# Attention followed by a mixture of experts: earlier row reads, weights in smaller pieces, and a sort that is cut differently

## The chip, the cores and the metric

One core of a Trainium2 chip. The metric is the device time of one execution in microseconds, lower is better. Times of a kernel are the median of several executions; the profile is one more execution with the hardware profiler on.

## What is computed

Two blocks after each other, all in float32: attention over 8 batches, 8 heads, 576 positions and 64 dimensions, with a causal mask and a bias from the running sum of `s`; then a mixture of 8 experts over the 4608 tokens of 512 elements that this gives. A token takes the expert of its own highest logit, or, where its local gate is at least 0.5, that of the token before.

```python
scores = scale * np.matmul(q, k.transpose(0, 1, 3, 2))
cum = np.cumsum(np.maximum(s, 0.0), axis=-1)
bias = -(cum[:, :, :, None] - cum[:, :, None, :])
scores = np.where(causal, -1e9, scores + np.minimum(bias, 0.0))
attn = softmax(scores)                       # exp, over its sum + 1e-9
x = matmul(attn, v)                          # to (B, S, 512)
logits = x @ w_gate                          # 8 experts
gate = sigmoid(x @ w_local)
for b, s:                                    # in order along s
    e = argmax(logits[b, s]) if s == 0 or gate[b, s] < 0.5 else prev_e
    prev_e = e
    p = softmax(logits[b, s])
    out[b, s] = p[e] * (np.maximum(x[b, s] @ w1[e], 0.0) @ w2[e])
```

## The kernel before

**Attention.** 32 steps, one for each pair of heads (n = 0 to 31, four for each batch), and a 33rd that ends the last. In step n TensorE computes the scores of pair n (L307, L313), ScalarE their exponentials (L318, L329), GpSimd the causal mask in place (L324, L331), and TensorE the values of pair n-1 (L359, L371, L375). The values carry nine more columns, so that logits and local gate come out of the same matmuls. VectorE divides by the sums and writes the token rows of the batch to the tiles `xb` and `xt` in SBUF (L365, L378). Loads of the batches are issued on SyncE's queue; `store` (L381) moves the rows of the last 64 positions of a batch into place, on the same queue.

**The sort.** The tokens have to be brought together by expert. `Group` does this for several batches at once, in five stages (choose, rows, hold, rank, gates), which give each token a row number in the DRAM tensor `x_rows`; then one indirect DMA from GpSimd for each 128 tokens (five a batch, the last with 64) scatters the rows there (L937). `plan` says after which half step of the attention each stage and scatter is issued: batches 0 to 2 from step 13, 3 to 5 from step 25, three scatters a half step. `Sort.early` (step 27) then fills the gap behind the rows so far of experts 0 to 3 with empty rows: their first 128 rows each can be worked on before the sort is finished. The last two batches are sorted after the attention, while the first blocks of the experts run: their stages and scatters are `hooks` (L112), which `experts` calls after so many groups of matmuls. `fill` (L767) writes 128 empty rows behind each expert's rows, eight DMAs on SyncE's queue, and `tables` computes which expert and which first row each further block has.

**The experts.** 41 blocks of up to 128 rows: 4 early ones and 37 further ones. Block i needs its rows (`xg`, 257 KB, read by GpSimd's queue, L999 for the early ones, L1003 else), which TensorE transposes (L1010, `turn_x`) and VectorE copies (L1012), and the two weight matrices of its expert (`w`, two loads of 2 MB on SyncE's queue, L947, 16 KB a partition each). Layer 1 is 32 matmuls of 128x128 (L1027; each matmul shows as two records), layer 2 is 8 of 128x512 (L1039). ScalarE and VectorE apply the relu, VectorE multiplies by the gate (`y`, L1044), and GpSimd scatters y to the output (L1045). There are three weight buffers: the first is allocated ahead of the attention, so that the first block's weights are loaded during it (step 20); the other two lie where the attention's tiles were. `xg` has four buffers.

Each engine works through its instructions in program order. The loop of the blocks sets that order:

```python
for i in range(NBL):
    load(i + 2)              # SyncE: weights
    layer1(i + 1, 0)
    fetch(i + 2)             # GpSimd: rows
    layer1(i + 1, 1)
    layer2(i)                # turn_x(i + 2) in its middle, the store of y at its end
```

So GpSimd's queue holds: store of block i-1, read of rows i+2, store of block i, read of rows i+3. A load of weights waits on SyncE's queue until TensorE has read the buffer for the last time. All stores go to one tensor, so each waits for the one before it to land.

Of the kernel before, what the change touches and what calls it, by code (L numbers as in the profile page):

```python
# [10 lines left out]
F32 = mybir.dt.float32  # L11
# [7 lines left out]
P = 128  # L19
# [32 lines left out]
@with_exitstack  # L52
def kernel(
    ctx: ExitStack,
    tc: tile.TileContext,
    q: bass.AP,
    k: bass.AP,
    vm: bass.AP,
    vt: bass.AP,
    vT: bass.AP,  # L60
    s: bass.AP,
    w_gate: bass.AP,
    w_local: bass.AP,
    w1: bass.AP,
    w2: bass.AP,
    out: bass.AP,
):
# [12 lines left out]
    recs = const.tile([P, NPAIR, 2 * NF + 1], F32, name="recs")  # L80
    out_of = const.tile([P, 1], I32, name="out_of")
    sort = Sort(tc, const, lg, rows_d, ident)

    with ExitStack() as main:
        keep = main.enter_context(tc.tile_pool(name="keep", bufs=4))
        wf = main.enter_context(tc.tile_pool(name="wf", bufs=1))
        xs = {}

        def new_x(b):
            xs[b] = keep.tile([P, NF, XW], F32, name="xb"), keep.tile([TL, XW], F32, name="xt")  # L90
            return xs[b]


        plan = {}

        def at(n, half, *what):
            plan.setdefault((n, half), []).extend(what)

        for bs, n0, each in (((0, 1, 2), 13, 3), ((3, 4, 5), 25, 3)):
            g = sort.group(bs, xs)  # L100
            for i, (n, half) in enumerate(((n0, 1), (n0 + 1, 0), (n0 + 1, 1), (n0 + 2, 0), (n0 + 2, 1))):
                at(n, half, g.stages[i])
            for i, f in enumerate(g.scatters):
# [12 lines left out]
        experts(tc, w1, w2, out, rows_d, ident, sort,  # L116
                [("early", e) for e in range(EARLY)] + [("further", i) for i in range(SURE)], hooks, wf, first)
    total = nc.values_load(sort.total[0:1, 0:1], min_val=0, max_val=NBLK,  # L118
                           skip_runtime_bounds_check_because="a count of blocks")
    with tc.If(total > SURE):  # L120
        experts(tc, w1, w2, out, rows_d, ident, sort, [("further", i) for i in range(SURE, SURE + 2)])
        with tc.If(total > SURE + 2):
            experts(tc, w1, w2, out, rows_d, ident, sort, [("further", i) for i in range(SURE + 2, NBLK)])
    wrong = nc.values_load(out_of[0:1, 0:1], min_val=0, max_val=P * NPAIR * (2 * NF + 1),
                           skip_runtime_bounds_check_because="a count of elements")
    with tc.If(wrong > 0):
        attention_general(tc, q, k, vm, vt, s, w_gate, w_local, cum_d, x_d, ident, lg)
        with ExitStack() as again:
            pool = again.enter_context(tc.tile_pool(name="again", bufs=1))
            ps = again.enter_context(tc.tile_pool(name="again_ps", bufs=3, space=PSUM))  # L130

            def bank(n):
                return [ps.tile([P, 512], F32, name="bank") for _ in range(n)]

            sort = Sort(tc, pool, lg, rows_d, ident)
            sort.constants(bank)
            for bs in (range(0, 4), range(4, 8)):
                xs = {b: (pool.tile([P, NF, XW], F32, name=f"xb{b % 4}"), pool.tile([TL, XW], F32, name=f"xt{b % 4}"))
                      for b in bs}
                for b in bs:  # L140
                    r0 = b * S
# [11 lines left out]
def attention(ctx, tc, q, k, vm, vt, vT, s, w_gate, w_local, ident, lg, recs, keep, new_x, plan):  # L153
# [787 lines left out]


def load_weights(nc, w, w1, w2, e):
    for a, src in ((0, w1), (DK * F, w2)):
        n = DK * F if src is w1 else FK * D
        s = src[e : e + 1] if isinstance(e, int) else src[bass.ds(e, 1)]
        nc.sync.dma_start(w[:, a : a + n], s.rearrange("o p c f -> (o p) (c f)"))  # L947


@with_exitstack  # L950
def experts(ctx, tc, w1, w2, out, rows_d, ident, sort, blocks, hooks=(), wf=None, first=None):

# [19 lines left out]
    ws, xg, at, xT, hT = {0: first} if wf else {}, {}, {}, {}, {}  # L972

    def bank(n):
        return [ps_r.tile([P, 512], F32, name="bank") for _ in range(n)]
# [17 lines left out]
    def fetch(i):  # L993
        if i >= NBL or i in xg:
            return
        kind, j = blocks[i]
        xg[i] = gp.tile([P, XW], F32, name="xg")
        if kind == "early":
            nc.gpsimd.dma_start(xg[i], rows_d[j * R : j * R + P, :])  # L999
        else:  # L1000
            row = nc.values_load(sort.rowi[0:1, j : j + 1], engines=[ET.Pool], min_val=0, max_val=E * R,  # L1001
                                 skip_runtime_bounds_check_because="a block's first row")
            nc.gpsimd.dma_start(xg[i], rows_d[bass.ds(row, P), :])  # L1003

    def turn_x(i):
        if i >= NBL:
# [27 lines left out]
    def layer2(i):  # L1034
        ps = ps_y.tile([P, D], F32, name="yp")
        h = hT.pop(i)
        w = ws[i][:, DK * F :].rearrange("p (c d) -> p c d", c=FK)
        for c in range(FK):
            mm(ps, lhsT=h[:, c, :], rhs=w[:, c, :], start=(c == 0), stop=(c == FK - 1))  # L1039
# [4 lines left out]
        nc.vector.tensor_scalar_mul(y, ps, xg[i][:, D + 1 : D + 2])  # L1044
        nc.gpsimd.indirect_dma_start(  # L1045
            out=out[:, :], out_offset=bass.IndirectOffsetOnAxis(ap=at[i][:, 0:1], axis=0),
            in_=y[:, :], element_offset=0, bounds_check=N - 1, oob_is_err=False, in_offset=None)

    for i, (kind, _) in enumerate(blocks):
        if kind == "early" or i < 2:  # L1050
            fetch(i)
    load(0)
    load(1)
    turn_x(0)
# [47 lines left out]
```

## Time and profile before

Median of three runs 1109.63 us (1104.3 to 1112.8). The profiled execution spans 1120.1 us, with a mean granted TensorE clock of 0.951.

| engine | busy, us | share of the span |
|---|---|---|
| TensorE matmuls | 968.3 | 86% |
| TensorE weight loads (beside the matmuls) | 710.3 | 63% |
| VectorE | 210.6 | 19% |
| ScalarE | 181.8 | 16% |
| GpSimd | 173.9 | 16% |

| DMA issue | count | KB each | median us to landing |
|---|---|---|---|
| expert weights | 82 | 2048 | 13.5 |
| row reads | 41 | 257 | 11.4 |
| stores of y (indirect) | 41 | | 8.7 |
| scatters of full tiles (indirect) | 32 | | 3.7 |

A row of the busy view by stretches gives for each engine the time in which it had an instruction running; the rest of the stretch is idle. The granted clock is the share of full speed that TensorE was given. In the view of waits, a line names the engine and line that stood still, what ended the wait, and the total, the number of times and the longest. In the timeline, the brackets hold the idle time of the engine just before the row and what ended it.

### The profile page before, as it was taken

How to read it: one execution, taken by the hardware profiler on the slowest of the kernel's cores; microseconds unless marked ns; L12 is line 12 of the kernel's file. 1: busy time of each engine (PE TensorE's matmuls, PEld its weight loads, DVE VectorE, ACT ScalarE, POOL GpSimd, SP SyncE). 2: the span in 40 equal slices, each digit the busy share in tenths (PEclk: the TensorE clock that was granted, in tenths of full speed). 3: DMA queues.
4: the chain of work that ended last, by engine and by line, in shares of the span. 5: the costliest groups of instructions: out<-in, count | busy, mean ns of one | idle time of the engine just before them, and what ended most of it. 6: DMA issues, size and time to landing. Idle time of an engine off the chain costs nothing.

```text
span 1120.1 us, 16042 instructions
## 1 busy us (share of the span) xinstructions
PE 968.3 (86%) x6538; PEld 710.3 (63%) x6538; DVE 210.6 (19%) x649; ACT 181.8 (16%) x465; POOL 173.9 (16%) x333
## 2 busy tenths in 40 slices
PE   8999998999989978888888787878888897879785
PEld 6778877777877645565556565656555564646462
DVE  3222352223424211111111111111111111111110
ACT  4444444445530000000000000000000000000000
POOL 2212215312451211010001010101000010101000
PEclk9999999999998989999999999899999888999898
DMA  9435436653229965857575757575757475766640
GB/s 281 134 115 175 148 89 208 261 159 114 95 87 362 349 268 192 322 202 285 199 318 198 308 203 298 194 308 197 295 195 310 183 267 235 264 243 246 252 180 18
DMA packets 42646, 245.24 MB, mean 219 GB/s; under 512 B 17309, under 2 KB 17341, under 8 KB 29376
## 3 DMA queue, kind: packets, MB, share of 16 engines
q1 hardware_dynamic: 31024, 213.36, 51.2%
q0 software_dynamic: 9632, 29.73, 7.1%
q10 hardware_dynamic: 1904, 0.98, 0.3%
q8 instruction: 56, 0.92, 0.3%
q14 instruction: 30, 0.25, 0.1%
HBM read 220.67 MB, written 23.64 MB: 218 GB/s over the span
## 4 chain that ended last, share of the span: by engine, by line
issue 33%; DMA 29%; PE 2%; POOLq 1%; POOL 0%; DVE 0%
DMA out_dram<-y,at 28%; PE yp L1039 2%; DMA xg<-x_rows 1%; POOLq L1001 1%; PE hp L1027 1%; POOL out_dram L1045 0%; POOL x_rows L937 0%; DVE y L1044 0%; POOLq L1045 0%; PE xp L1010 0%; POOLq L118 0%; POOLq L1003 0%
## 5 line engine op out<-in xcount | busy, mean ns | idle before, releaser
L1039 PE MATMUL yp<-w,hT 128*128 128x512 f32 x656 | 329.5, 651 | 0.0
L1027 PEld LDWEIGHTS hp<-xT,w 128*128 128x128 f32 x2624 | 302.1, 193 | 22.7 <-issue 21.3
L1027 PE MATMUL hp<-xT,w 128*128 128x128 f32 x2624 | 303.6, 277 | 3.2 <-DMA w<-in_w_dram 2.3
L1039 PEld LDWEIGHTS yp<-w,hT 128*128 128x128 f32 x656 | 131.9, 211 | 141.6 <-issue 141.6
L318 ACT ACTIVATE sc<-ps,bias 128x320 f32<-128x320 f32 (+3 forms) x384 | 151.2, 487 | 159.2 <-PE ps L313 99.3
L359 PEld LDWEIGHTS po<-va,sc 128*128 128x128 f32 x1280 | 149.1, 193 | 24.8 <-issue 20.7
L359 PE MATMUL po<-va,sc 128*128 128x74 f32 x1280 | 158.4, 279 | 3.7 <-POOL sc L324 3.7
L1045 POOL DMA_INDIRECT out_dram<-y,at x41 | 40.8, 996 | 673.0 <-DVE y L1044 620.5
L1032 ACT ACTIVATE hT<-hp 128x512 f32<-128x512 f32 x41 | 24.5, 597 | 718.9 <-PE hp L1027 718.9
L1010 PE MATMUL xp<-ident,xg 128*128 128x128 f32 x164 | 30.0, 313 | 126.2 <-DMA xg<-x_rows 126.2
L1010 PEld LDWEIGHTS xp<-ident,xg 128*128 128x128 f32 x164 | 20.1, 157 | 157.0 <-issue 153.0
L307 PE MATMUL ps<-qk 64*128 64x320 f32 (+3 forms) x768 | 110.3, 406 | 0.3 <-ACT sct L329 0.3
L324 POOL TENSOR_SCALAR_AFFINE_SELECT sc<-sc 128x256 f32<-128x256 f32 (+1 forms) x96 | 47.4, 494 | 193.5 <-ACT sc L318 192.2
L1012 DVE COPY xT<-xp 128x512 f32<-128x512 f32 x41 | 28.3, 691 | 256.5 <-PE xp L1010 256.5
L1030 DVE TENSOR_SCALAR hT<-hp 128x512 f32<-128x512 f32 x41 | 28.4, 692 | 251.7 <-PE hp L1027 251.7
L307 PEld LDWEIGHTS ps<-qk 64*128 64x128 f32 x768 | 61.1, 187 | 18.1 <-issue 1.7
L1044 DVE TENSOR_SCALAR y<-yp,xg 128x512 f32<-128x512 f32 x41 | 30.8, 751 | 149.5 <-PE yp L1039 149.5
L363 DVE RECIPROCAL recs<-po 128x4 f32<-128x4 f32 x64 | 11.7, 183 | 185.9 <-PE po L359 185.9
L937 POOL DMA_INDIRECT x_rows<-xb,r_slot_i x32 | 31.5, 984 | 9.1 <-issue 8.0
L365 DVE TENSOR_TENSOR xb<-po,recs 128x256 f32<-128x256 f32 x64 | 27.2, 425 | 2.4
L371 PE MATMUL pot<-va,sc 128*64 128x74 f32 x512 | 23.5, 234 | 0.0
L1003 POOL DMA_DIRECT2D xg<-x_rows x37 | 21.9, 591 | 0.7 <-DMA w<-in_w_dram 0.7
(141 smaller groups left out, 258.3 us busy)
## 6 DMA issues: line engine op xcount, KB each, us to landing
w<-in_w_dram SPq DMA_DIRECT2D x82, 2048.0 KB, 13.5
xg<-x_rows POOLq DMA_DIRECT2D x41, 257.0 KB, 11.4
qk<-in_q_dram SPq DMA_DIRECT2D x7, 1152.0 KB, 5.0
qk<-in_k_dram SPq DMA_DIRECT2D x7, 1152.0 KB, 8.1
vTb<-in_vT_dram SPq DMA_DIRECT2D x7, 1152.0 KB, 9.8
va<-in_vm_dram SPq DMA_DIRECT2D x7, 1024.0 KB, 8.4
x_rows<-r_empty SPq DMA_DIRECT2D x13, 257.0 KB, 4.8
qk<-in_q_dram SPq DMA_DIRECT2D x4, 288.0 KB, 7.5
```

The source lines that it names most:

```text
L307: mm(ps[:, h, at : at + q1 - q0], lhsT=kb[d, hp, c * P : c * P + P], rhs=qb[d, hp, q0:q1], start=True, stop=True)
L318: nc.scalar.activation(sc[:, h, a:z], ps[:, h, a:z], Act.Exp, bias=bias[:, i : i + 1], scale=scale)
L324: nc.gpsimd.affine_select(out=x, in_=x, compare_op=Alu.is_ge, fill=0.0, base=0, pattern=[[0, 2], [0, len(diag)], [1, P]], channel_multipli ...
L359: mm(po[:, t % 2, h, :], lhsT=weights(n, c, t, h), rhs=va[:, c, 2 * hp + h, :], start=(c == 0), stop=(c == t))
L937: self.s.nc.gpsimd.indirect_dma_start(out=next(self.s.views)[:, :], out_offset=bass.IndirectOffsetOnAxis(ap=self.slot[:z, m : m + 1], axis=0),
L1010: tr(ps[:, c, :], xg[i][:, c * P : (c + 1) * P], ident)
L1012: nc.vector.tensor_copy(xT[i], ps)
L1027: mm(ps[:, j, :], lhsT=w[:, c, f], rhs=xT[i][:, c, :], start=(c == 0), stop=(c == DK - 1))
L1030: nc.vector.tensor_scalar_max(hT[i][:, g : g + 4], ps, 0.0)
L1039: mm(ps, lhsT=h[:, c, :], rhs=w[:, c, :], start=(c == 0), stop=(c == FK - 1))
L1044: nc.vector.tensor_scalar_mul(y, ps, xg[i][:, D + 1 : D + 2])
L1045: nc.gpsimd.indirect_dma_start(out=out[:, :], out_offset=bass.IndirectOffsetOnAxis(ap=at[i][:, 0:1], axis=0), in_=y[:, :], element_offset= ...
```

## The change

Seven edits. (1) Rows are read three blocks ahead instead of two, from a pool of five buffers of their own. (2) The weights of a block are loaded in eight pieces of 4 KB a partition instead of two of 16 KB. (3) The stores are declared as disjoint, so that none waits for another. (4) The groups of the sort are batches 0 and 1 (from step 9), 2 to 4 (from step 21) and 5 to 7 (after the attention). (5) Two scatters a half step instead of three. (6) The rows of the four early blocks are read in step 30 of the attention, on SyncE's queue, before the loads of weights. (7) One value tile of the attention (`va0`) moves next to the tile `vTb`, and the last batch's `store` goes to ScalarE's queue, so that the second block's weights neither need a tile that is used to the end nor stand behind that store. The aim is that reads, loads and stores of the experts are asked for earlier and hold each other up less.

```diff
-        for bs, n0, each in (((0, 1, 2), 13, 3), ((3, 4, 5), 25, 3)):
+        for bs, n0 in (((0, 1), 9), ((2, 3, 4), 21)):
             g = sort.group(bs, xs)
-            for i, (n, half) in enumerate(((n0, 1), (n0 + 1, 0), (n0 + 1, 1), (n0 + 2, 0), (n0 + 2, 1))):
-                at(n, half, g.stages[i])
+            for f, i in zip(g.stages, (1, 2, 3, 4, 4)):
+                at(n0 + i // 2, i % 2, f)
             for i, f in enumerate(g.scatters):
-                at(n0 + 3 + i // each // 2, i // each % 2, f)
+                i = 5 + i // 2
+                at(n0 + i // 2, i % 2, f)
         at(3, 1, sort.constants)
-        at(27, 1, sort.early)
-        first = wf.tile([P, DK * F + FK * D], F32, name="w")
-        at(20, 0, lambda bank: load_weights(nc, first, w1, w2, 0))
-        last = sort.group((6, 7), xs)
+        at(28, 1, sort.early)
+        gx = main.enter_context(tc.tile_pool(name="gx", bufs=5))
+        ready = {"w": {0: wf.tile([P, DK * F + FK * D], F32, name="w")}, "x": {}}
+        at(20, 0, lambda bank: load_weights(nc, ready["w"][0], w1, w2, 0))
+
+        def fetch_early(bank):
+            for e in range(EARLY):
+                ready["x"][e] = gx.tile([P, XW], F32, name="xg")
+                nc.sync.dma_start(ready["x"][e], rows_d[e * R : e * R + P, :])
+
+        at(30, 0, fetch_early)
+        last = sort.group((5, 6, 7), xs)
...
     p_vT = pool("p_vT", 1)
+    p_va = pool("p_va", 1)
     p_in = pool("p_in", 2)
...
-    vas = [once.tile([P, NF, H, VW], F32, name=f"va{i}") for i in range(2)]
+    vas = [(once if i else p_va).tile([P, NF, H, VW], F32, name=f"va{i}") for i in range(2)]
...
-            nc.sync.dma_start(row[:, h], xs[b, "t"][h * TL : h * TL + TL])
+            (nc.sync if b < B - 1 else nc.scalar).dma_start(row[:, h], xs[b, "t"][h * TL : h * TL + TL])
...
-        nc.sync.dma_start(w[:, a : a + n], s.rearrange("o p c f -> (o p) (c f)"))
+        s = s.rearrange("o p c f -> (o p) (c f)")
+        for i in range(0, n, F):
+            nc.sync.dma_start(w[:, a + i : a + i + F], s[:, i : i + F])
...
+    outs = dram_disjoint_views(out[:, :], NBL)
...
-        xg[i] = gp.tile([P, XW], F32, name="xg")
-        if kind == "early":
-            nc.gpsimd.dma_start(xg[i], rows_d[j * R : j * R + P, :])
-        else:
-            row = nc.values_load(sort.rowi[0:1, j : j + 1], engines=[ET.Pool], min_val=0, max_val=E * R,
+        xg[i] = gx.tile([P, XW], F32, name="xg")
+        row = nc.values_load(sort.rowi[0:1, j : j + 1], engines=[ET.Pool], min_val=0, max_val=E * R,
...
-            out=out[:, :], out_offset=bass.IndirectOffsetOnAxis(ap=at[i][:, 0:1], axis=0),
+            out=outs[i][:, :], out_offset=bass.IndirectOffsetOnAxis(ap=at[i][:, 0:1], axis=0),
...
-        fetch(i + 2)
+        fetch(i + 3)
```

More of the change, by code (lines that the diff above doesn't have):

```diff
@@ L116 @@
         experts(tc, w1, w2, out, rows_d, ident, sort,
-                [("early", e) for e in range(EARLY)] + [("further", i) for i in range(SURE)], hooks, wf, first)
+                [("early", e) for e in range(EARLY)] + [("further", i) for i in range(SURE)], hooks, wf, gx, ready)
     total = nc.values_load(sort.total[0:1, 0:1], min_val=0, max_val=NBLK,
@@ L946, in load_weights, with experts @@
         s = src[e : e + 1] if isinstance(e, int) else src[bass.ds(e, 1)]
-        nc.sync.dma_start(w[:, a : a + n], s.rearrange("o p c f -> (o p) (c f)"))
+        s = s.rearrange("o p c f -> (o p) (c f)")
+        for i in range(0, n, F):
+            nc.sync.dma_start(w[:, a + i : a + i + F], s[:, i : i + F])
 @with_exitstack
-def experts(ctx, tc, w1, w2, out, rows_d, ident, sort, blocks, hooks=(), wf=None, first=None):
+def experts(ctx, tc, w1, w2, out, rows_d, ident, sort, blocks, hooks=(), wf=None, gx=None, ready=None):
     nc = tc.nc
@@ L971, in experts @@
     ps_r = pool("ps_r", 3, space=PSUM)
-    ws, xg, at, xT, hT = {0: first} if wf else {}, {}, {}, {}, {}
+    gx = gx or pool("gx", 5)
+    ws, xg = (ready["w"], ready["x"]) if ready else ({}, {})
+    at, xT, hT = {}, {}, {}
+    outs = dram_disjoint_views(out[:, :], NBL)
     def bank(n):
@@ L995, in fetch @@
             return
-        kind, j = blocks[i]
-        xg[i] = gp.tile([P, XW], F32, name="xg")
-        if kind == "early":
-            nc.gpsimd.dma_start(xg[i], rows_d[j * R : j * R + P, :])
-        else:
-            row = nc.values_load(sort.rowi[0:1, j : j + 1], engines=[ET.Pool], min_val=0, max_val=E * R,
-                                 skip_runtime_bounds_check_because="a block's first row")
-            nc.gpsimd.dma_start(xg[i], rows_d[bass.ds(row, P), :])
+        j = blocks[i][1]
+        xg[i] = gx.tile([P, XW], F32, name="xg")
+        row = nc.values_load(sort.rowi[0:1, j : j + 1], engines=[ET.Pool], min_val=0, max_val=E * R,
+                             skip_runtime_bounds_check_because="a block's first row")
+        nc.gpsimd.dma_start(xg[i], rows_d[bass.ds(row, P), :])
     def turn_x(i):
@@ L1045, in layer2 @@
         nc.gpsimd.indirect_dma_start(
-            out=out[:, :], out_offset=bass.IndirectOffsetOnAxis(ap=at[i][:, 0:1], axis=0),
+            out=outs[i][:, :], out_offset=bass.IndirectOffsetOnAxis(ap=at[i][:, 0:1], axis=0),
             in_=y[:, :], element_offset=0, bounds_check=N - 1, oob_is_err=False, in_offset=None)
-    for i, (kind, _) in enumerate(blocks):
-        if kind == "early" or i < 2:
-            fetch(i)
     load(0)
     load(1)
+    if not ready:
+        for i in range(3):
+            fetch(i)
     turn_x(0)
```

## The prediction

> **What bounds the kernel now.** I read the page's 40 slices first. TensorE is busy nearly everywhere, which hides more than it tells, but from slice 12 on its digit falls from 9 to 8 and the granted clock is no longer steady.
>
> ```profile
> PE   8999998999989978888888787878888897879785
> PEclk9999999999998989999999999899999888999898
> DMA  9435436653229965857575757575757475766640
> ```
>
> So I cut the span where the code changes stage: the attention ends at 332.9 us, the first layer 2 of the experts starts at 359.3, and from 407.47 on the blocks repeat. The busy view over these stretches (columns: length, then busy time with instruction count for each engine, granted clock, DMA share, GB/s):
>
> ```profile
> 0.00:332.90 332.90, 323.12 (x3069) 258.71 (x3071) 106.17 (x426) 156.47 (x422) 98.57 (x234) 0.99 0.48 156
> 332.90:359.30 26.40, 21.75 (x161) 20.10 (x162) 10.50 (x40) 2.04 (x4) 2.52 (x6) 0.81 0.91 363
> 359.30:407.47 48.17, 39.31 (x190) 25.68 (x190) 10.62 (x34) 1.19 (x2) 12.82 (x17) 0.93 0.80 284
> 407.47:1107.50 700.03, 584.13 (x3123) 405.78 (x3121) 82.56 (x151) 22.09 (x37) 59.03 (x75) 0.94 0.63 243
> ```
>
> The last row is 700 us long, with 116 us in which TensorE does nothing. The waits of that stretch name one cause for nearly all of it: the transposes of a block's rows wait for the row read, 36 times, 3.2 us each.
>
> ```profile
> PE xp L1010 <- DMA xg<-x_rows: 115.9, 36, 4.2
> ```
>
> The timeline of one block shows how the wait arises:
>
> ```profile
> 612.26 7.31 PE L1027 MATMUL hp<-xT,w 128*128 128x128 f32 x64
> 612.45 18.59 SPq L947 DMA_DIRECT2D w<-in_w_dram  x4
> 612.46 0.75 DVE L1044 TENSOR_SCALAR y<-yp,xg 128x512 f32<-128x512 f32 x1 [4.38 <-PE yp L1039]
> 613.49 0.99 POOL L1045 DMA_INDIRECT out_dram<-y,at  x1 [17.61 <-DVE y L1044]
> 614.48 0.59 POOL L1003 DMA_DIRECT2D xg<-x_rows  x1
> ...
> 619.40 3.60 PE L1039 MATMUL yp<-w,hT 128*128 128x512 f32 x8
> ...
> 626.08 0.63 PE L1010 MATMUL xp<-ident,xg 128*128 128x128 f32 x4 [3.08 <-DMA xg<-x_rows]
> ...
> 626.54 3.60 PE L1039 MATMUL yp<-w,hT 128*128 128x512 f32 x8
> ```
>
> GpSimd issues the read of rows (L1003) only after the store before it on its queue, and that store waits for y of the block just ended. The read is issued 2.2 us after layer 2 ends and lands 11.4 us later (the DMA issues' median). TensorE has only 10.6 us of work until it needs the rows (layer 1 from 612.26 to 619.40, half of layer 2 to 622.84), so it stops for 3 us. The page's chain puts 28% on the stores instead, since each store also waits for the one before. That store landed at 622.3 and its successor went out at 631.21, right after its y: in the repeating part the wait on the store costs nothing.
>
> The same idle time costs a second time. Windows of 4 us around the longest wait:
>
> ```profile
> 392.00:396.00 4.00, 2.41 (x6) 0.76 (x4) 0.00 (x0) 0.00 (x0) 1.58 (x2) 1.00 1.00 430
> 396.00:400.00 4.00, 0.00 (x0) 0.00 (x0) 0.00 (x0) 0.00 (x0) 0.00 (x0) 0.93 0.81 338
> 400.00:404.00 4.00, 3.06 (x7) 1.91 (x8) 0.75 (x2) 0.00 (x0) 0.00 (x0) 0.50 0.01 2
> ```
>
> After 6.5 us without matmuls the clock is 0.50 for some 4 us. Shorter stops do it at times: the half layer 2 at 607.12 after a stop of 2.86 us took 5.30 us, and after 3.08 us at 626.54 only 3.60.
>
> [...] stops of 2.8 to 4.2 us halve it in some blocks and not in others, and stretches without stops (48 to 188 us) stay at 1.00. [...]
>
> **The change part by part.**
>
> *Reads three ahead.* The read of block i+3 is now issued where that of i+2 was. It keeps its 2.2 + 11.4 = 13.6 us, and has one block more until it is needed: 10.6 + 14.5 = 25.1 us. The stop goes, and with it the half clock. What is left is TensorE's own work at full clock, from the block above: layer 1 7.14, two halves of layer 2 of 3.44, transposes 0.46, together 14.48 us a block. From 407.47 there are 37 layer 1, 38 layer 2 and 36 transposes: 37 x 7.14 + 38 x 6.88 + 36 x 0.46 = 542 us. I add 4 us for small waits: 546 for 700, so -154 us (116 of stops, the rest clock).
>
> *Weights in pieces.* 8 DMAs a block for 2. One issue on SyncE takes 0.43 us (two in 0.86), so 8 take 3.4 us of a 14.5 us period on a queue that does nothing else; the first four, for w1, are out in 1.7 us. The bytes are the same: 4.19 MB of weights, 0.26 read and 0.26 stored per block. Whether they fit in 14.48 us: loads with 9 KB a partition ran at 440 GB/s (216 to 224 us), the mixed start with slices of 2.3 KB and less at 312 (8 to 12 us). 4 KB lies between: 10.7 to 15.1 us for 4.72 MB. I take 400 GB/s, 11.8 us, which hides behind TensorE; the slow end gives a period of 15.1, +23 us. Loads still start when layer 2 three blocks back ends, 14.5 us before w1 and 21.6 us before w2 is needed; landings were 13.5 us in the median, w1 earlier than w2.
>
> *Stores apart, five row buffers.* Nothing in the repeating part. At the start it counts: the second store went out at 393.03 although its y was ready near 382, because the first, issued at 373.62, landed at 392.8 behind ten scatters. The row read of block 4 stood behind it (394.68), and TensorE stopped 6.53 us. In the new order that read comes after the first store alone.
>
> *Last group of three batches.* 15 scatters for 10 after the attention: 5 x 1.27 = 6.4 us more on GpSimd, and 1.2 MB more to move while the 2.1 MB of empty rows and the weights of block 3 move. This is a new cost. The scatters then start about 8 us earlier (next item), so they end near 371 as before. The read of block 4 goes out at 376 to 386 instead of 394.7. From 359.3 to 407.47 there are 36.3 us of work at full clock; I leave 7 us of stops (bounds 2 and 14) against 11.9 now: -5.
>
> *Early rows and weights.* Rows of the four early blocks are read during the attention. The 3.8 us wait at 333 goes, and with it the half clock from 336 to 345. The 26.4 us stretch becomes 2.0 for transposes and copy, 3.6 + 0.5 + 3.6 + 7.14 of TensorE, and some 1.5 of the sort's small matmuls and waits: 18.4, so -8. The second block's weights no longer wait for the end of the attention, and the last store moves to ScalarE's queue, which has nothing urgent for some 8 us. The four reads on SyncE wait for the fill; behind them stands only that load, with time in hand.
>
> *Scatters thinner.* The waits of the whole span hold one stop in the attention:
>
> ```profile
> PE po L359 <- POOL sc L324: 3.7, 1, 3.7
> ```
>
> At 188 us three scatters in a row (3.8 us) held GpSimd while TensorE waited for the mask (L324), and the clock stayed at 0.50 to about 198. Two at a time take 2.5 us. Only one of the two groups shows this stop, so I take -6, bounds 0 and -8.
>
> Sum: -154 - 5 - 8 - 6 = -173 us; from the median of 1109.6 that is **937 us**.
>
> **Rivals.** (A) The wait moves to the weights: SyncE's loads become the bound, at a period of 15.5 to 16.5 us because pieces, row reads and stores disturb each other more in less time. For it: DMA share is 0.63 over 18.7 us, that is 11.8 us a block, or 0.81 of the new period. Against: weights stopped TensorE once, for 2.3 us, in the crowded start. At 16.0: 37 x 1.5 = +56, near 993. (B) Slower: pieces cost so much that DMA falls to the 0.225 MB/us seen with 256-byte slices; 4.72 MB then take 21 us against 18.7 now, 37 x 2.3 = +85, near 1195. Against: 4 KB is far from 256 bytes. (C) The repeating part gains, the start loses: 15 scatters, fill and weights jam, and block 4 starts 15 us later than I think: near 955.
>
> **How the numbers follow.** Forecast 0.65; A 0.15; C 0.17; B 0.03. The low end adds up the favourable bounds: 4 us of small waits less, 5 less in the start, 2 less in the attention and 4 in the handover: 15 us, 922. The high end takes in C, the slow pieces (+23) and the near half of A: 972. Faster by over 1% holds for the forecast, A and C: 0.95, taking 0.02 off for errors in all of them. Within 1%: 0.02. Slower: 0.03.
>
> **What would show it.** Right: the wait of the transposes for rows is gone from the repeating part; layer 1 starts about 14.5 us apart; the clock stays at 1.00 past the start; DMA share near 0.8. In the attention no half clock near 190 us. The row reads may still take 11 us to land: it no longer matters. Wrong: TensorE's waits name the weights in many blocks (A), loads land later than 15 us (B), or the half clock returns without stops. The wait for rows of block 4 tells how far C holds.

## The result and the profile after

The changed kernel takes 968.2 us (median of four, 966.5 to 969.7) where the kernel before takes 1109.3: a ratio of 0.873, with a 95% interval from 0.869 to 0.877. The forecast was 937 us. The direction and the size of the main gain came as predicted; 31 us did not.

The 40 slices of the changed kernel:

```profile
PE   8999998999979996999999999999999999999995
PEclk8999998999979998999999999999999999999998
DMA  9463262637541658988988988988988988988950
```

Counted from 0, TensorE and its clock show a 9 in every slice from 16 to the last but one, where the kernel before showed eights and sevens. Three dents lie ahead: at slice 6 (145 to 169 us) and, deeper, 11 (265 to 289), both in the attention, and at 15 (362 to 386), in the first blocks. The same stages as in the prediction, cut at the first transpose of rows, at the first layer 2, at layer 1 of block 4 and at the end of the last layer 2 (columns as there: length, busy time of TensorE, its weight loads, VectorE, ScalarE and GpSimd, granted clock, DMA share, GB/s):

```profile
0.00:342.40 342.40, 327.54 (x3072) 261.32 (x3072) 104.88 (x426) 156.64 (x422) 94.06 (x229) 0.97 0.51 162
342.40:362.14 19.74, 18.32 (x159) 17.10 (x158) 10.60 (x37) 2.07 (x4) 0.00 (x0) 1.00 0.70 247
362.14:411.24 49.10, 40.30 (x191) 26.46 (x190) 11.10 (x35) 1.19 (x2) 18.37 (x25) 0.90 0.90 307
411.24:952.50 541.26, 541.26 (x3123) 394.06 (x3121) 82.49 (x151) 22.09 (x37) 58.51 (x74) 1.00 0.86 313
```

The fourth row settles the largest claim. In 541.26 us TensorE is busy for 541.26 us, at clock 1.00. The groups of instructions on the page give the transposes no idle time ahead of them (last columns: busy time, mean of one in ns, idle before it):

```profile
L1023 PE MATMUL xp<-ident,xg 128*128 128x128 f32 x164 | 24.7, 273 | 0.0
```

One block of the repeating part in the timeline:

```profile
599.79 6.86 PE L1040 MATMUL hp<-xT,w 128*128 128x128 f32 x60
600.07 32.12 SPq L960 DMA_DIRECT2D w<-in_w_dram  x22
600.58 0.99 POOL L1058 DMA_INDIRECT out_dram<-y,at  x1 [12.87 <-DVE y L1057]
601.56 0.59 POOL L1016 DMA_DIRECT2D xg<-x_rows  x1
...
606.49 3.60 PE L1052 MATMUL yp<-w,hT 128*128 128x512 f32 x8
...
609.92 0.60 PE L1023 MATMUL xp<-ident,xg 128*128 128x128 f32 x4
...
613.79 7.31 PE L1040 MATMUL hp<-xT,w 128*128 128x128 f32 x64
```

The read at 601.56 still goes out 2 us after layer 2 ends, behind the store. But the transposes at 609.92 carry no bracket: the rows that they take were asked for one block earlier. The next layer 1 starts at 613.79; the median distance of two is 14.45 us. (The view begins at 600, inside a layer 1: four of its 64 records lie ahead.) By engine, the page's chain of waits is now TensorE's:

```profile
PE 79%; DMA 2%; issue 2%; POOL 1%; DVE 1%; POOLq 0%; DVEq 0%
```

### The profile page after: what moved, and what is told of

It reads as the page before. It is cut to its first block, busy times and chain, and to the rows that moved or that the text cites. A ratio compares the mean times of both kernels' runs of the same rounds, so it can differ in the third digit from the quotient of the medians.

```text
span 964.8 us, 16728 instructions
## 1 busy us (share of the span) xinstructions
PE 927.7 (96%) x6538; PEld 698.9 (72%) x6538; DVE 209.8 (22%) x649; ACT 182.0 (19%) x465; POOL 171.9 (18%) x329
## 4 chain that ended last, share of the span: by engine, by line
PE 79%; DMA 2%; issue 2%; POOL 1%; DVE 1%; POOLq 0%; DVEq 0%
PE hp L1040 31%; PE yp L1052 29%; PE po L369 8%; PE ps L317 5%; DMA x_rows<-xb,r_slot_i 2%; PE xp L1023 2%; PE pot L381 1%; PE pot L385 0%; PE vwp L284 0%; PE ps L323 0%; POOL x_rows L947 0%; PE bank L876 0%; POOL sc L334 0%; PE vwt L296 0%; PE ltp L407 0%
## 5 line engine op out<-in xcount | busy, mean ns | idle before, releaser
L1052 PE MATMUL yp<-w,hT 128*128 128x512 f32 x656 | 295.5, 594 | 0.0
L1052 PEld LDWEIGHTS yp<-w,hT 128*128 128x128 f32 x656 | 119.0, 191 | 119.6 <-issue 119.4
L317 PE MATMUL ps<-qk 64*128 64x320 f32 (+3 forms) x768 | 113.9, 417 | 0.0
L317 PEld LDWEIGHTS ps<-qk 64*128 64x128 f32 x768 | 63.2, 193 | 18.2 <-issue 2.9
L373 DVE RECIPROCAL recs<-po 128x4 f32<-128x4 f32 x64 | 11.7, 183 | 185.9 <-PE po L369 183.5
L1023 PE MATMUL xp<-ident,xg 128*128 128x128 f32 x164 | 24.7, 273 | 0.0
```

The lines of the kernel that those rows point to most:

```text
L317: mm(ps[:, h, at : at + q1 - q0], lhsT=kb[d, hp, c * P : c * P + P], rhs=qb[d, hp, q0:q1], start=True, stop=True)
L1023: tr(ps[:, c, :], xg[i][:, c * P : (c + 1) * P], ident)
```

## Where the 31 us went

The stages of all kernels that ran, from the profiled executions ("attention" runs to the first transpose of rows; the rest of the span, 12 to 13 us, is the end). The names say what was edited, and the sections after the table show how. Each ratio is to the kernel before as it ran beside that kernel. Its medians there went from 1109 to 1117 us, so rows are better compared by the ratio than by the microseconds, and ratios less than about 0.01 apart are not told apart here:

| kernel | us, median | ratio to before | attention | handover | start | repeating |
|---|---|---|---|---|---|---|
| before | 1109.3 | 1 | 336.9 | 22.4 | 48.1 | 700.0 |
| after | 968.2 | 0.873 | 342.4 | 19.8 | 49.1 | 541.6 |
| after, rows two ahead | 993.2 | 0.898 | 348.6 | 19.8 | 49.7 | 560.0 |
| after, 16 KB weights | 977.9 | 0.876 | 348.4 | 19.8 | 54.1 | 541.6 |
| after, stores as one tensor | 973.1 | 0.872 | 352.9 | 21.3 | 44.5 | 541.6 |
| after, old cut of the sort | 948.6 | 0.858 | 329.7 | 19.8 | 42.6 | 541.6 |
| after, 128 small instructions more | 976.0 (one run) | | 350.4 | 21.4 | 48.9 | 541.6 |
| before, rows three ahead | 958.9 | 0.861 | 336.4 | 21.9 | 41.5 | 541.6 |
| before, 4 KB pieces | 976.2 | 0.876 | 341.1 | 21.1 | 43.8 | 557.2 |
| pairs of batches | 946.2 | 0.856 | 328.1 | 19.8 | 42.4 | 541.6 |
| pairs, 16 KB weights | 947.2 | 0.849 | 328.9 | 19.8 | 42.2 | 541.6 |
| pairs, stores as one tensor | 947.8 | 0.848 | 329.5 | 21.4 | 44.1 | 541.6 |
| pairs, both of these | 947.7 | 0.850 | 328.9 | 19.8 | 42.6 | 541.6 |
| the last, empty rows on ScalarE's queue | 953.8 | 0.855 | 329.5 | 19.8 | 47.3 | 541.6 |

Four things stand out. The repeating part is 541.6 us in every kernel whose reads are three ahead, whatever else differs. Kernels with the changed kernel's attention code spread over 342 to 353 us there; with the old cut or with pairs it is 328 to 330 (the three rows with 336 to 341 include the wait for the early rows). The start goes from 41.5 to 54.1. And the kernel before with the lead of the reads alone, at 0.861 (0.855 to 0.867), is faster than the changed kernel with all seven edits, at 0.873 (0.869 to 0.877): taken together, the other six edits cost more than they brought. With the old cut of the sort back it is 0.858.

## The experiments: the lead of the reads against the size of the pieces

The prediction gave all 154 us of the repeating part to the lead of the reads and nothing to the pieces. Four kernels make the square of the two.

```diff
# after, rows two ahead
-        for i in range(3):
+        for i in range(2):
...
-        fetch(i + 3)
+        fetch(i + 2)
```

> The changed kernel with the row reads two blocks ahead as before, all else as changed. Theory (the lead of the read is what removed the stops): the read lands 11 us after its issue as before, TensorE stops about 3 us a block again, a block takes 17 to 18.7 us, in all 1070 to 1110 us. Rival (the pieces of 4 KB let a row read through in 6 to 8 us): it lands before it is needed at 10.6 us, a block stays at 14.5 us, in all 965 to 980 us.

Measured: 993.2 us (ratio 0.891 to 0.905), in neither range but much nearer to the rival. The period is 14.97 us in the median. The waits of this kernel name the rows, but little of them:

```profile
PE xp L1023 <- DMA xg<-x_rows: 14.4, 18, 2.8
```

14.4 us in 18 waits, where the kernel before lost 115.9 in 36. With pieces, reads that are asked for two blocks ahead nearly suffice. The other three:

```diff
# before, rows three ahead (the whole edit)
-        xg[i] = gp.tile([P, XW], F32, name="xg")
+        xg[i] = gp.tile([P, XW], F32, name="xg", bufs=5)
...
-        if kind == "early" or i < 2:
+        if kind == "early" or i < 3:
...
-        fetch(i + 2)
+        fetch(i + 3)
# before, 4 KB pieces (the whole edit; the reverse of it is "after, 16 KB weights")
-        nc.sync.dma_start(w[:, a : a + n], s.rearrange("o p c f -> (o p) (c f)"))
+        s = s.rearrange("o p c f -> (o p) (c f)")
+        for i in range(0, n, F):
+            nc.sync.dma_start(w[:, a + i : a + i + F], s[:, i : i + F])
```

> The kernel before with one edit: the row reads are issued one block earlier, into five buffers. Theory (as the prediction had it): the stops of 3 us and their half clock go, the repeating part falls from 700 to about 542 us (period 14.45 to 14.6), the rest stays near 407, total 945 to 970. Rival (the pieces are needed as well, since the reads beside 16 KB rows take longer once the period is shorter): stops of over 1 us stay, the repeating part is above 580 us, total above 990.

> The kernel before with one edit: weights in 4 KB pieces, the rows still two ahead. The read has 10.6 us until TensorE needs it. If the pieces alone let it land earlier, as the changed kernel with the reads two ahead suggests: landing in about 9 to 10 us, waits for rows of 10 to 25 us in all instead of 116, repeating part 555 to 570, total 965 to 990. Rival (it took the pieces and the untracked stores together, or the early rows): the stops stay at 2 to 3 us a block, total above 1050.

> The changed kernel with the weights loaded again in two DMAs of 16 KB rows a block; the reads stay three ahead. Theory (the lead of the read alone takes the stop away: 11 us to land, 25 us of time): the period stays at 14.45 us and the repeating part at 541 to 545 us, no wait of the transposes for rows, total 960 to 975. Rival (the pieces are what lets reads through; with 16 KB rows in a shorter period the DMA engines clog): period above 15 us, total above 985. On the trickle of single instructions in the start: if it comes from the burst of pieces beside the scatters, it is gone here, and the start takes some 8 us less (near 41); if from the scatters and the fill alone, it is still there (near 49).

Measured: 958.9 us (ratio 0.855 to 0.867) for the lead alone, 976.2 (0.870 to 0.883) for the pieces alone, 977.9 (0.869 to 0.882) for the changed kernel with 16 KB weights. The first two came out as expected, except that with the pieces alone the reads landed in 8.1 us, sooner than the 9 to 10 expected. In the third the period stayed at 14.45 as the theory said, but the total is 3 us above its range and the start took 54.1 us: the trickle of single instructions described below is gone, and TensorE waits 9.5 us for the rows of block 4 instead. So that half of the expectation, 8 us less, was a miss.

The issue lists of three kernels show what the pieces do (last column: median us from issue to landing). Before, with the lead alone:

```profile
w<-in_w_dram SPq DMA_DIRECT2D x82, 2048.0 KB, 13.2
xg<-x_rows POOLq DMA_DIRECT2D x41, 257.0 KB, 11.3
```

Before, with the pieces alone:

```profile
w<-in_w_dram SPq DMA_DIRECT2D x328, 512.0 KB, 9.3
xg<-x_rows POOLq DMA_DIRECT2D x41, 257.0 KB, 8.1
DMA packets 78076, 245.30 MB, mean 251 GB/s; under 512 B 21245, under 2 KB 21277, under 8 KB 75296
```

And the packet line of the kernel before:

```profile
DMA packets 42646, 245.24 MB, mean 219 GB/s; under 512 B 17309, under 2 KB 17341, under 8 KB 29376
```

Before, 42646 - 29376 = 13270 packets are of 8 KB and more; with pieces 2780. The difference, 10490, is close to the number of the weights' rows: 82 loads of 128 rows of 16 KB make 10496. A row of weights is one packet, and the trace's medians for one are 611 ns at 16 KB and 159 ns at 4 KB. The row read has 64 packets of some 4 KB (160 ns each) and the store ahead of it on its queue up to 64, over 16 engines: together up to 8 an engine. How far apart they go out stands in the traces of the kernels before and after, the one with 16 KB rows of weights and the other with 4 KB. In the repeating part the commonest distance below 1 us between two packets of one row read is 764 ns before and 312 after, and 156 or 157 ns after the start of a packet of the read one of the weights starts, for 2262 of 2304 packets before and 2019 of 2240 after. Over 8 packets the pieces save, as an estimate from these distances, 8 x (764 - 312) ns = 3.6 us. Measured: 11.4 - 8.1 = 3.3. That this is the cause is argued from these numbers. A rival, that it counts how many bytes of weights one DMA asks for and not how long a packet is, was not tested apart. That the read lands 3.3 us earlier, and that it follows from cutting the loads and not from another edit, is shown.

That was just what was missing. Two blocks ahead, the read has 10.6 us until TensorE needs the rows, of which 2.2 pass before it is issued: 2.2 + 11.4 = 13.6 leaves a stop of 3, and 2.2 + 8.1 = 10.3 leaves none, or a short one now and then. So either edit alone takes away most of the stops, and the second of them adds little: of 158 us that the lead is worth alone, it is worth 18 once the pieces are there (560.0 against 541.6). The pieces are worth 143 alone (700.0 against 557.2) and nothing beside the lead.

One more edit was put back on the same question: the stores tracked as one tensor.

```diff
# after, stores as one tensor
-    outs = dram_disjoint_views(out[:, :], NBL)
...
-            out=outs[i][:, :], out_offset=...
+            out=out[:, :], out_offset=...
```

> The changed kernel with the stores tracked as one tensor again, so that each store waits for the one before. Theory: nothing in the repeating part (a store lands in one period), 541 us; in the start the second store, and the row read of block 4 behind it, wait for the first to land, so 0 to 6 us more there; total 966 to 976. Rival (a store beside the denser loads takes longer than the 14.45 us of a period, so the queue of GpSimd falls behind and the lead of the reads is used up): period above 14.8 us, total above 985.

Measured: 973.1 us (ratio 0.864 to 0.880), the repeating part the same. The start is 44.5 us, shorter and not longer as expected: the trickle described below is gone, and TensorE waits 5.5 us for weights instead. The chain of stores costs nothing measurable, in the repeating part or in the start: with the reads three ahead, the read of block 4 already stands in front of the second store (issued at 407.4 and 408.3 us here).

## The experiments: the cut of the sort

Two stops in the attention of the changed kernel, from its waits:

```profile
DVE xb L375 <- DMA x_rows<-xb,r_slot_i: 8.6, 1, 8.6
PE ltp L407 <- DVE lb L375: 6.7, 1, 6.7
PE po L369 <- POOL sc L334: 3.8, 2, 2.5
```

The third line holds one stop of each group of scatters. In the first group, GpSimd's part of the timeline:

```profile
150.15 0.99 POOL L947 DMA_INDIRECT x_rows<-xb,r_slot_i  x1 [0.17 <-issue]
151.45 0.97 POOL L947 DMA_INDIRECT x_rows<-xb,r_slot_i  x1 [0.30 <-issue]
152.43 0.44 POOL L334 TENSOR_SCALAR_AFFINE_SELECT sc<-sc 128x256 f32<-128x256 f32 x1
```

Two scatters stand ahead of the mask. TensorE waits from 150.4 to 152.9 us for it, and the clock falls to 0.50 before that wait is over. Windows of 4 us:

```profile
148.00:152.00 4.00, 2.38 (x22) 2.00 (x18) 0.71 (x3) 2.50 (x8) 2.20 (x4) 0.93 0.12 40
152.00:156.00 4.00, 3.08 (x12) 2.62 (x14) 0.00 (x0) 0.00 (x0) 3.49 (x6) 0.50 0.51 182
156.00:160.00 4.00, 4.00 (x32) 2.99 (x30) 0.18 (x1) 1.89 (x4) 1.18 (x4) 0.72 0.09 17
```

In the second group the same wait lasts 1.3 us, but a larger one follows:

```profile
265.58 1.11 PE L369 MATMUL po<-va,sc 128*128 128x74 f32 x8 [1.26 <-POOL sc L334]
273.41 0.35 PE L407 MATMUL ltp<-lt,fold 128*64 128x9 f32 x2 [6.72 <-DVE lb L375]
```

The token tiles `xb` have four buffers, so batch 6 writes where batch 2 stood. In the new cut batch 2 belongs to a group that starts at step 21, and its scatters are issued from step 23; batch 6 begins at step 24. VectorE has to wait at 264 us until the scatter has read the tile (8.6 us), and TensorE waits for VectorE. Windows of 4 us:

```profile
264.00:268.00 4.00, 1.43 (x11) 1.14 (x10) 0.09 (x1) 0.44 (x2) 3.39 (x5) 0.94 0.90 210
268.00:272.00 4.00, 0.00 (x0) 0.00 (x0) 0.00 (x0) 0.00 (x0) 0.77 (x2) 0.50 1.09 279
272.00:276.00 4.00, 2.59 (x10) 1.48 (x10) 0.68 (x3) 0.76 (x2) 1.65 (x3) 0.50 0.10 25
```

Two kernels test that the cut is what costs:

```diff
# after, old cut of the sort
-        for bs, n0 in (((0, 1), 9), ((2, 3, 4), 21)):
+        for bs, n0, each in (((0, 1, 2), 13, 3), ((3, 4, 5), 25, 3)):
...   (stages, pace of the scatters and early as before)
-        last = sort.group((5, 6, 7), xs)
+        last = sort.group((6, 7), xs)
# pairs of batches
-        for bs, n0 in (((0, 1), 9), ((2, 3, 4), 21)):
+        for bs, n0, each in (((0, 1), 9, 1), ((2, 3), 17, 1), ((4, 5), 25, 2)):
...
-                i = 5 + i // 2
+                i = 5 + i // each
...
-        last = sort.group((5, 6, 7), xs)
+        last = sort.group((6, 7), xs)
```

> The changed kernel with the sort cut as before: batches 0-2 from step 13, 3-5 from step 25, three scatters a half step, 6-7 after the attention; all else as changed. Theory (the new cut costs what the prediction missed): the stops near 150 and 270 us go, the attention ends at 333 to 335 us instead of 342.4; ten scatters instead of fifteen after it, so layer 1 of block 2 no longer trickles and the stretch from the first layer 2 to the repeating part takes 40 to 43 us instead of 49.1; in all 950 to 954 us. Rival (the stops come from the pieces of the weights or from the moved tiles): the attention still ends near 342 and the time stays within 3 us of 968.

> The changed kernel with the sort in four groups of two batches (from steps 9, 17 and 25, the last after the attention), one scatter a half step in the first two groups, two in the third. Theory (a token tile is written again before its scatter has landed at 270 us, two scatters ahead of a mask at 150 us): both stops go, since a tile's scatters now end three steps before its reuse; the attention ends at 326 to 330 us, the start of the experts is that of ten scatters, in all 940 to 948 us. Rival (any scatter beside the loads of a batch delays the mask, however few): stops of 1 to 3 us remain at three places, the attention ends at 336 or later, 955 to 965 us.

Measured: 948.6 us (ratio 0.854 to 0.863) with the old cut, 946.2 (0.852 to 0.861) with pairs. Neither has a wait for the mask or for a token tile among its waits of over 1 us. With pairs the theory held. With the old cut, time and attention came out a little better than its theory had them, but one part was a miss: the trickle of single instructions in layer 1 of block 2 is shorter, not gone. The slices of the kernel with pairs have no dent at 6 or 11:

```profile
PE   8999999999999998999999999999999999999994
PEclk9999999999999999999999999999999999999998
DMA  9473254639614679989889889899898898898950
```

The new cut of the sort, that is edits 4 and 5 together, made the kernel some 20 us slower than it would have been without it (16 by the ratios, 19 in the profiles): 12.7 us in the attention (342.4 against 329.7) and 6.5 in the start (49.1 against 42.6). In the attention TensorE stands idle 14.9 us with the new cut and 6.1 with the old, and is busy 327.5 and 323.6 us: 8.8 us of stops and 3.9 of slower work. That nothing else of the cut plays a part wasn't separated. The attention with the new cut takes up to 353 us in other kernels with the same code, so this share varies from run to run. The kernel with pairs is 22 us below the changed kernel; its own share over the old cut, 2 us, isn't told apart from noise.

The number of scatters in a row is not what decides by itself. With the old cut back, three stand ahead of a mask again, from 184.5 to 188.0 us, and TensorE doesn't wait, while the kernel before stopped for 3.7 us at the same place in the program: there the three began 4 us later, at 188.4, after GpSimd itself had waited 7.4 us for ScalarE. Why ScalarE is later there wasn't separated.

## The experiments: the start

In the start of the changed kernel layer 1 of block 2 comes apart:

```profile
379.93 0.38 PE L1040 MATMUL hp<-xT,w 128*128 128x128 f32 x1 [1.15 <-issue]
382.03 0.37 PE L1040 MATMUL hp<-xT,w 128*128 128x128 f32 x1 [1.72 <-issue]
384.12 0.37 PE L1040 MATMUL hp<-xT,w 128*128 128x128 f32 x1 [1.72 <-issue]
386.21 0.37 PE L1040 MATMUL hp<-xT,w 128*128 128x128 f32 x1 [1.72 <-issue]
```

Its last 17 records take from 375.7 us until layer 2 starts at 388.6; at the pace of the repeating part, 7.14 us for 64, they would take 1.9. Ten of them are spread out, four as shown, and with the weight loads between them the instructions start in steps of some 0.7 us ("the trickle"). The last seven follow closely from 386.9. The clock falls meanwhile, though no stop in it is longer than 1.72 us:

```profile
376.00:380.00 4.00, 1.23 (x7) 0.57 (x5) 0.00 (x0) 0.00 (x0) 3.08 (x4) 1.00 0.98 273
380.00:384.00 4.00, 0.68 (x2) 0.68 (x3) 0.00 (x0) 0.00 (x0) 3.08 (x4) 0.52 1.04 384
384.00:388.00 4.00, 1.81 (x7) 1.37 (x7) 0.00 (x0) 0.60 (x1) 0.25 (x1) 0.50 1.03 414
```

"issue" says that the profile shows nothing that TensorE waited for. Fifteen scatters are issued from 364.4 to 383.0, the empty rows before 372.8, and then the pieces of block 3's weights. Is it a place in TensorE's stream of instructions, or the traffic? A kernel with 128 small instructions more at the beginning moves the place:

```diff
# after, 128 small instructions more
+    for i in range(32):
+        mm(idle[:32, 1, :1], lhsT=ident[:, :32], rhs=ident[:, :1], start=True, stop=True)
```

> The changed kernel with 32 tiny matmuls (128 instructions on TensorE) added at the very start, which fall partly into time in which TensorE waits there; they write a scratch bank that nothing reads. It asks why layer 1 of block 2 trickles from 375 to 387 us, one instruction every 0.70 us. Theory I (TensorE runs out of instructions at a fixed place of its stream, and the refill stands behind the transfers): the trickle starts 128 instructions earlier in the program, in layer 2 of block 0 or the start of layer 1 of block 2, or it is gone. Theory B (the burst of scatters, empty rows and weights slows TensorE itself while it lasts): it stays on the second half of layer 1 of block 2, some 11 to 15 us after the first scatter. Time 966 to 975 us under B; 955 to 970 under I.

Measured: 976.0 us in its one run, and the trickle at nearly the same records of the same layer, the last 18, from 385.4 to 397.5. It does not follow the position in the stream. Nor does the changed kernel's DMA view of 372 to 388 us have any packet of an instruction queue (the whole trace has 92). That is against theory I; that the traffic is what slows TensorE, as theory B says, is not shown by it. The trickle appeared in all five kernels with pieces and separate stores, and in none of the five others so far. So pieces and separate stores were put back one at a time and both, with pairs:

> Groups of two batches as in the run with pairs, weights in 16 KB rows again. The repeating part stays at 541.6 us (the reads three ahead have time to spare). In the start the trickle of single instructions went with the pieces in every run so far: without them it should be gone. Theory: the ten scatters leave the row read of block 4 enough time, the start takes 38 to 43 us and the total is 938 to 947. Rival (16 KB rows hold up the scatters in the start, as with fifteen of them): a wait for the rows of block 4 of 3 to 10 us, start 44 to 52, total 948 to 958.

> Groups of two batches, pieces, but stores tracked as one tensor. The trickle showed in all five runs with pieces and stores apart, in none of the two with pieces and stores as one. If the stores' tracking decides it: no trickle here, a wait for weights of up to 4 us instead, start 39 to 43 (with pairs and stores apart: 42.4), total 941 to 949. If it is chance or the burst of pieces alone: TensorE again runs single instructions 0.7 us apart for some 4 us, start 42 to 46, total 945 to 952. Attention 328 and repeating part 541.6 in both.

> Groups of two batches, 16 KB weight rows, stores as one tensor: of the change only the reads three ahead, the early rows and weights and the sort's new places are left, with pairs. Theory: pieces and separate stores are worth nothing once the reads are three ahead, so the total is that of the run with pairs, 940 to 950, repeating part 541.6, start 38 to 44, no trickle. Rival (one of the two was needed beside the denser traffic): period above 14.7 us or a stop of over 5 us for the rows of block 4, total above 952.

Measured: 947.2 us (ratio 0.845 to 0.852), 947.8 (0.845 to 0.852) and 947.7 (0.845 to 0.854). There is no trickle in any of the three; the theories held, but for one start 1.1 us longer than expected. And the start is no shorter for it: 42.2, 44.1 and 42.6 us, against 42.4 with the trickle. In its place stands a wait for the weights of block 3, here with both edits put back:

```profile
374.32 3.94 PE L1038 MATMUL hp<-xT,w 128*128 128x128 f32 x20 [3.77 <-DMA w<-in_w_dram]
```

So with ten scatters the trickle is not the bound of the start: without it TensorE stands for the same 4 us a block later. (With fifteen, the two kernels without it have starts of 44.5 and 54.1 us, against 48.9 to 49.7 with it.) How pieces and separate stores together make TensorE issue one instruction at a time stays open. With pairs and the reads three ahead, neither edit is worth anything that can be measured.

The weights of block 3 are issued at 358.7 us, behind eight writes of empty rows on SyncE's queue. The last kernel takes them from behind those:

```diff
# pairs, both put back, empty rows on ScalarE's queue
-            nc.sync.dma_start(next(self.views)[bass.ds(row, P), :], self.empty)
+            (nc.scalar if late else nc.sync).dma_start(next(self.views)[bass.ds(row, P), :], self.empty)
```

> Groups of two batches, 16 KB weight rows, stores as one tensor, and the eight writes of empty rows after the sort issued on ScalarE's queue instead of SyncE's, so that the weights of block 3 no longer stand 8.7 us behind them. Theory (the one stop left in the start, 3.8 us for the weights of block 3, comes from that place in the queue): the weights go out near 352 instead of 358.7 us, the stop falls below 1 us, the start takes 38.5 to 40.5 us instead of 42.6, total 942 to 946. Rival (the same bytes have to move before block 3 in any order: empty rows, ten scatters and weights share the DMA engines): the stop stays at 3 to 4 us or moves to the rows of block 4, start 42 to 45, total 946 to 951.

Measured: 953.8 us (ratio 0.849 to 0.862). What the rival said happened, by more than it said: the stop moved to the rows of block 4. Start (47.3 us) and total lie above both ranges. The weights go out at 356.8 us and not at 352, since their buffer is free only when layer 2 of block 0 has ended (353.19 + 3.60 us). Asked for 1.9 us sooner and no longer in one queue with the empty rows, they land in time: that stop is gone. But one of 8.2 us for the rows of block 4 has come. By the profile their read waits for the empty rows to land, and goes out at 385.4 instead of 379.3:

```profile
385.38 0.61 POOL L1014 DMA_DIRECT2D xg<-x_rows  x1 [20.86 <-DMA x_rows<-r_empty]
387.54 1.02 POOL L1056 DMA_INDIRECT out_dram<-y,at  x1 [1.55 <-DMA out_dram<-y,at]
```

This reads as a competition of the transfers in the start: what is let through sooner pushes back what stood ahead of it, and in this order the rows lose more than the weights gain. The number of scatters may count for the same reason: with ten, the start took 41.5 to 44.1 us in seven kernels (47.3 with the empty rows moved, 48.1 in the kernel before), with fifteen 44.5 to 54.1 in five.

## Why the prediction was right, and where it was off

On the profiled executions, which the steps were read from, the forecast was 1120.1 - 173 = 947.1 us and the result is 964.8: 17.7 too much. The measured 968 us lies just under the high end of the range, 972. That end was made of rival C, slow pieces and part of rival A. Only a part of C came, some 6 us in the start; the pieces were not slow, and weights stopped nothing in the repeating part. What filled the range was the attention (15.5 us) and the reckoning (14 us, below), which the range did not name: that it holds is partly luck. The large gain was not luck: its mechanism is the one that was forecast. By the steps:

- **Reads three ahead: right, and 5 us better.** 541.3 us for 546 with small waits and 542 without. The forecast of 14.48 us a block measured 14.45, and the clock came back to 1.00 as soon as the stops went. The step's claim that this edit alone does it is borne out by the kernel with nothing else changed, 541.6.
- **Weights in pieces: no cost, as taken; one part of the working failed.** The estimate of 11.8 us of DMA time a block was near: a share of 0.86 of 14.45 us is 12.4 (with 16 KB rows 0.81, or 11.7). (The 440 GB/s in its working, from 216 to 224 us, came with 171 packets of 16 KB and 78 of 9, not with 9 KB alone.) "The bytes are the same" was right too, yet the step treated landing times as fixed: the read "keeps its 2.2 + 11.4". The pieces shorten the landing of a row read, to 8.1 us, and this edit alone is worth 143 us in the repeating part. How long a packet of weights is, 159 ns for 611, wasn't in the working. Since the lead hides the read anyway, the total did not suffer.
- **Stores apart: the cause was misnamed.** The earlier read of block 4 was put down to the separate stores. The kernel before with the lead alone has a start of 41.5 us with its stores in one tensor, and the changed kernel with one tensor has 44.5: it is the lead that puts the read of block 4 ahead of the second store. The time was wrong too: that read went out at 394.0 us, where 376 to 386 was forecast. No stop came of it: the trickle had held TensorE back, and the rows were needed only at 407.4.
- **Last group of three batches: mis-sized.** Forecast -5 us, measured +0.9 (49.1 against 48.2): 6 us. No wait for the rows of block 4 was left, but the trickle in layer 1 of block 2 takes its place, 12.9 us for 1.9 of work. In effect this is rival C at less than half its size; that a jam of scatters, empty rows and weights is the cause is not shown, since the trickle's cause is open. Without the new cut the start gains 5.6 (42.6).
- **Early rows and weights: right.** 19.7 us for 18.4, with the clock at 1.00.
- **Scatters thinner: failed.** Forecast -6, measured +9.5, 15.5 us off. Two scatters still held the mask long enough: the clock was halved in a stop of 2.5 us. And three need not hold it, as the kernel with the old cut shows. The other stop wasn't in the working at all: the step asked who waits for GpSimd behind the scatters, and not who waits to overwrite what they read.

The sum: 15.5 in the attention, 1.3 in the handover, 5.9 in the start, -4.7 in the repeating part and -0.3 at the end make 17.7. The other 14 us lie in the reckoning. The gain was read from a profile of 1120.1 us and taken off a median of 1109.6, 10.5 lower, and the profile after is 3.4 below its own median. The kernel before has stops that halve the clock at times, and its executions differ by chance (1104 to 1113 us beside the changed kernel). In the runs beside the other kernels its longer executions show the lower clocks, from 1102.0 us at 0.964 to 1124.7 at 0.943. The profiled one, at 0.951, was a long one and had more to lose. Building the time up from what remains by the same steps, 326.9 + 18.4 + 43.2 + 546 and 12.6 for the end, gives 947.

The prediction names stops of 2.8 to 4.2 us that halve the clock in some blocks. These traces show it halved by shorter ones. The clock was at 0.50 from 151.5 us on, before the stop of 2.5 us at 150 us was over, and in the trickle it was 0.52 from 380 to 384 us and 0.50 from 384 to 388, with no single stop longer than 1.72. The length of a stop does not decide by itself: in the kernel before one of 2.86 us halved the clock and one of 3.08 did not. That it stays at 1.00 where there are no stops was right: in the 541 us of the repeating part it did.

## What to carry to other kernels

A read that lands too late can be asked for sooner or be let through faster, by smaller packets in the stream beside it; either may suffice, and the second one brings little (700.0 us here, 541.6 by the one, 557.2 by the other, 541.6 by both). Try the edit that the argument rests on by itself: here it was faster alone than with six more. When the moment of a transfer *out of* a tile is moved, look for the next writer of that tile and count its buffers, even in a stage that the edit is not about. And take a forecast from what remains after the change, stage by stage, rather than a gain in one profiled execution off the median of others.

## What was not expected of the hardware

- Beside a stream of 16 KB packets (611 ns each) a row read of 257 KB landed in 11.4 us, beside 4 KB packets (159 ns) in 8.1. With the reads three ahead, the repeating part moved 313 GB/s with either size.
- The clock fell to half in the middle of a stop of 2.5 us, and in a stretch of many stops of at most 1.72 us.
- In the crowded start of the changed kernel TensorE took 12.9 us for its last 17 records of a layer, 0.76 us each, with no wait in the records. Stretches like it came only where pieces and separate stores came together (five of five kernels, none of the other nine). What it waited for isn't shown.
